# Attention with pooled keys and a mixture of adapters: the tail's last two chunks finished in halves, the last normalise in one piece

## The chip, the cores and the metric

The kernel runs on one core of a Trainium2 chip. The core has TensorE (PE) for matrix products, VectorE (DVE), ScalarE (ACT) and GpSimd (POOL) for elementwise work, and SyncE (SP), which issues most transfers; transfers run on 16 DMA engines. The metric is the device time of one execution in microseconds. The kernel before took 407.74 us, the median of four runs between 407.55 and 408.02.

## The reference

Two steps run one after the other. Keys and values are the same tensor: `kv` averaged over blocks of 4 x 4 positions and multiplied by `w_sr`. There are 4 batches of 12288 queries with 768 keys, all of width 128.

```
kv_pool = kv.reshape(B, H//4, 4, W//4, 4, C).mean(axis=(2, 4))
k = v = kv_pool.reshape(B, -1, C) @ w_sr
a = softmax(q @ k.T / sqrt(C));  x = (a @ v).reshape(B*S, C)

logits = x @ w_gate                         # 8 experts
topk, w = two largest logits, softmax over the two
out = x + sum over the two: w * ((x @ A[e]) @ B[e])     # rank 16
```

The output is 49152 x 128 in float32, 25 MB.

## The kernel before, in words

The queries are cut into 96 chunks of 512 rows, numbered 0 to 95; in the tail K stands for 95. A chunk has S = 4 slices of 128 rows, one row per partition. Chunks pass through these steps, each a function of the program:

- `scores`: TensorE multiplies the keys with 512 queries, ACT takes the exponential into `em` (L246).
- `attend`: for each slice, TensorE sums six products of `em` with `vx`, which holds 128 value columns, 8 columns of values already multiplied by `w_gate`, and a column of ones. The result in PSUM therefore holds the unscaled output, the unscaled logits and the row sum, 137 columns a slice.
- `normalize`: DVE takes the reciprocal of the row sums (L258) and multiplies the 4 x 136 other columns with it (L263). The result `xn` holds x and the logits.
- `top` and `route`/`gates`: DVE finds the largest logits (MAX8, L281), POOL and ACT form the gate weights `gw`; the softmax over two is written with a tanh (L312).
- `transposes`/`turn_x`: TensorE transposes x, a copy brings it out of PSUM.
- `down`, `gate`, `up`: the product with all eight A matrices side by side (128 columns), the multiplication by `gw` into `hg` on DVE, a transpose of `hg`, and the product with all B matrices.
- `finish`: DVE adds x (L360), SP issues the store of 256 KB.

The main loop works on several chunks at once, so that TensorE always has another chunk's product to do. The order is written out by hand: `keep` holds each instruction in program order on its engine, and a scheduler adds only the waits. Each engine works through its own list in order, so an instruction that waits holds up everything behind it on that engine. Pools of buffers recycle: an instruction that writes into a recycled buffer waits until the last reader of its former content is done. The pool of output buffers `osb` has 6 buffers, that of `tt1` 3, the PSUM pool `ps_m` 2 banks.

After the loop stands the tail, straight code for what is left of chunks K-4 to K. It spreads the work over the engines with its own helpers. `turn_x` and `turn_h` transpose into a PSUM bank, `fetch` copies the bank with ACT (L514), `down_into` and `up_into` multiply into a given bank. An output is finished in one of two ways: `carry` copies the bank to SBUF with ACT (L552) and `add_there` adds x on POOL and stores through SP (L556, L557), which is used for K-4 and K-3; `add_here` adds on DVE and stores through the queue it is given (L547, L548), which is used for K-2, K-1 and K.

Around the change, chunk K is treated apart. Its attention sum lies in the PSUM tile `o95`. The reciprocal is at L587; ACT scales two of its slices (L590), DVE scales the 8 logits of all slices into a tile of their own, `lg` (L593), and then the other two slices (L595). Its routing runs on DVE (L600 to L607, L620) with a tanh on ACT (L617). `gate_part` forms `hg` for a part of a chunk (L562): K-1 whole, ahead of K, and K in two halves of two slices. K-1's `hg` is turned and fetched whole; K's is turned in two halves, of which ACT copies one (L635) and DVE the other (L637). K-1 is then added and stored whole, and K in two halves, the first through ACT's queue and the second through SP's.

Of the kernel before, what the change touches and what calls it, by code (L numbers as in the profile page):

```python
# [10 lines left out]
FP32 = mybir.dt.float32  # L11
BF16 = mybir.dt.bfloat16
U16 = mybir.dt.uint16
FP16 = mybir.dt.float16
AF = mybir.ActivationFunctionType
ALU = mybir.AluOpType
# [4 lines left out]
def kernel(  # L21
# [10 lines left out]
    nc = tc.nc  # L32
    P = 128
    B, N, C = q.tensor.shape
    E, RK = 8, 16
# [3 lines left out]
    T = 512  # L39
    S = T // P  # L40
    GC = 4
    GT = GC * T
    VC = C + E
# [3 lines left out]
    scale = 1.0 / float(np.sqrt(C))  # L47
# [7 lines left out]
    xpool = ctx.enter_context(tc.tile_pool(name="xpool", bufs=5))  # L55
    rpool = ctx.enter_context(tc.tile_pool(name="rpool", bufs=4))
    gpool = ctx.enter_context(tc.tile_pool(name="gpool", bufs=6))
    run = ctx.enter_context(tc.tile_pool(name="run", bufs=3))
# [3 lines left out]
    ps_a = ctx.enter_context(tc.tile_pool(name="ps_a", bufs=1, space=bass.MemoryType.PSUM))  # L62
    ps_m = ctx.enter_context(tc.tile_pool(name="ps_m", bufs=2, space=bass.MemoryType.PSUM))

    keep = tc.keep_in_program_order

    def mm(*a, **k):
        return keep(nc.tensor.matmul(*a, **k))  # L68

    def mtile(shape, dtype=FP32, name="mb"):  # L70
        return ps_m.tile(shape, dtype, tag="mb", name=name)
# [71 lines left out]
    id_bf = const.tile([P, P], BF16)  # L143
# [90 lines left out]
    em, acc, xn, xg, srt, gw = {}, {}, {}, {}, {}, {}  # L234
    tts, xT, hgT, hp, hg, dp = {}, {}, {}, {}, {}, {}
# [20 lines left out]
    def normalize(k):  # L256
        ri = rpool.tile([P, S], FP32, tag="rinv", name="rinv")
        keep(nc.vector.reciprocal(ri, acc[k][:, :, VC]))  # L258
        k0, m = first[k], k - first[k]
        if m == 0:  # L260
            xg[k0] = xpool.tile([P, GC, S, VC], FP32, tag="xn", name="xn")
        x = xg[k0][:, m]
        keep(nc.vector.tensor_tensor(x, acc[k][:, :, 0:VC],  # L263
                                     ri.unsqueeze(2).broadcast_to([P, S, VC]), op=ALU.mult))
        xn[k] = x
# [129 lines left out]
    b_bf = const.tile([P, C], BF16)  # L395
# [21 lines left out]
    for k in range(LA, NCHUNK):  # L417
        b, i = divmod(k, NB)
# [70 lines left out]
    K = NCHUNK - 1  # L489
    assert kh == [K - 3] and ku == [K - 4], (kh, ku)  # L490

    def bank(pool):
        if pool is ps_m:
            return mtile([P, S, P], name="tail_ps")
        if pool is ps_a:
            return ps_a.tile([P, S, 256], FP32, tag="acc", name="acc")
        return ps_s.tile([P, 2, T], FP32, tag="sg", name="sg")
# [8 lines left out]
    def turn_h(k, pool):  # L506
        ps = bank(pool).bitcast(BF16).rearrange("p a b -> p (a b)")[:, 0:T].rearrange("p (s c) -> p s c", s=S)
        for s in range(S):
            mm(ps[:, s], hg[k][:, s], id_bf, is_transpose=True, start=(s == 0), stop=(s == S - 1))
        hgT[k] = ps  # L510

    def fetch(which, k):
        sb = run.tile([P, S, P], BF16, tag="tt1", name="tt1")
        keep(nc.scalar.copy(sb, which[k]))  # L514
        which[k] = sb

    def tanhs():
        for rest_ in later:
            rest_()
        later.clear()  # L520
# [7 lines left out]
    def wide(o):  # L528
        return o.rearrange("p a b -> p (a b)")[:, 0:T].rearrange("p (s c) -> p s c", s=S)
# [6 lines left out]
    def up_into(k, o):  # L536
        dp[k] = o
        for s in range(S):
            mm(o[:, s], hgT[k][:, s], b_bf, start=(s == 0), stop=(s == S - 1))

    def dest(k):
        return out[k // GC * GT:(k // GC + 1) * GT].rearrange("(p j) c -> p j c", p=P)[
            :, k % GC * S:(k % GC + 1) * S]

    def add_here(k, lo, hi, queue):
        osb = opool.tile([P, S, C], FP32, tag="osb", name="osb")[:, 0:hi - lo]
        keep(nc.vector.tensor_tensor(osb, dp[k][:, lo:hi], xn[k][:, lo:hi, 0:C], op=ALU.add))  # L547
        keep(queue.dma_start(dest(k)[:, lo:hi], osb))  # L548
# [6 lines left out]
    def add_there(k):  # L555
        keep(nc.gpsimd.tensor_tensor(dp[k], dp[k], xn[k][:, :, 0:C], op=ALU.add))  # L556
        keep(nc.sync.dma_start(dest(k), dp[k]))  # L557

    def gate_part(k, lo, hi):
        if lo == 0:  # L560
            hg[k] = run.tile([P, S, P], BF16, tag="hg", name="hg")
        keep(nc.vector.tensor_tensor(  # L562
            hg[k][:, lo:hi].rearrange("p s (e r) -> p (s e) r", e=E),
            hp[k][:, lo:hi].rearrange("p s (e r) -> p (s e) r", e=E),
            gw[k][:, lo:hi].rearrange("p s e -> p (s e)")
            .unsqueeze(2).broadcast_to([P, (hi - lo) * E, RK]), op=ALU.mult))
# [3 lines left out]
    o95 = bank(ps_s).rearrange("p a (b c) -> p (a b) c", c=256)  # L570
# [12 lines left out]
    gate_part(K - 2, 0, S)  # L583
    add_there(K - 4)

    ri = rpool.tile([P, S], FP32, tag="rinv", name="rinv")
    keep(nc.vector.reciprocal(ri, o95[:, :, VC]))  # L587
    xn[K] = xpool.tile([P, GC, S, VC], FP32, tag="xn", name="xn")[:, 0]
    for s in range(2):
        keep(nc.scalar.activation(xn[K][:, s, 0:C], o95[:, s, 0:C], AF.Copy, bias=0.0,  # L590
                                  scale=ri[:, s:s + 1]))
    lg = rpool.tile([P, S, E], FP32, tag="lg", name="lg")
    keep(nc.vector.tensor_tensor(lg, o95[:, :, C:VC], ri.unsqueeze(2).broadcast_to([P, S, E]),  # L593
                                 op=ALU.mult))
    keep(nc.vector.tensor_tensor(xn[K][:, 2:S, 0:C], o95[:, 2:S, 0:C],  # L595
                                 ri[:, 2:S].unsqueeze(2).broadcast_to([P, 2, C]), op=ALU.mult))
    tanhs()
    so = rpool.tile([P, S, 8], FP32, tag="so", name="so")
    for s in range(S):
# [8 lines left out]
                                 op=ALU.is_ge))  # L608
# [6 lines left out]
    fetch(xT, K)  # L615
    th = rpool.tile([P, S, E], FP32, tag="th1", name="th1")
    keep(nc.scalar.activation(th, arg, AF.Tanh, bias=0.0, scale=0.5))  # L617
    gate_part(K - 1, 0, S)
    gw[K] = gpool.tile([P, S, E], FP32, tag="gw1", name="gw1")
    keep(nc.vector.scalar_tensor_tensor(gw[K], th, 1.0, mask, op0=ALU.add, op1=ALU.mult))  # L620
    down_into(K, ps_s)
    fetch(hgT, K - 2)
    carry(K - 3)
    add_there(K - 3)
    gate_part(K, 0, 2)
    gate_part(K, 2, S)
    up_into(K - 2, wide(bank(ps_s)))
    turn_h(K - 1, ps_m)
    fetch(hgT, K - 1)
    ps = bank(ps_m).bitcast(BF16).rearrange("p a b -> p (a b)")[:, 0:T].rearrange("p (s c) -> p s c", s=S)  # L630
    hgT[K] = run.tile([P, S, P], BF16, tag="tt1", name="tt1")
    for lo in (0, 2):
        for s in range(lo, lo + 2):
            mm(ps[:, s], hg[K][:, s], id_bf, is_transpose=True, start=(s == lo), stop=(s == lo + 1))
    keep(nc.scalar.copy(hgT[K][:, 0:2], ps[:, 0:2]))  # L635
    add_here(K - 2, 0, S, nc.sync)
    keep(nc.vector.tensor_copy(hgT[K][:, 2:S], ps[:, 2:S]))  # L637
    up_into(K - 1, bank(ps_m))
    dp[K] = wide(bank(ps_a))
    for lo in (0, 2):  # L640
        for s in range(lo, lo + 2):
            mm(dp[K][:, s], hgT[K][:, s], b_bf, start=(s == lo), stop=(s == lo + 1))
    add_here(K - 1, 0, S, nc.sync)
    add_here(K, 0, 2, nc.scalar)
    add_here(K, 2, S, nc.sync)


# [28 lines left out]
```

The softmax here doesn't subtract the row's maximum and nothing guards it: scores larger than these inputs give would overflow.

## Time and profile before

| What | Value |
|---|---|
| median of four runs | 407.74 us (407.55 to 408.02) |
| the profiled execution: time | 407.72 us |
| the profiled execution: span, first to last instruction | 405.7 us |
| TensorE busy | 379.3 us, 94% of the span |
| DVE, ACT, POOL busy | 325.0, 292.2, 170.4 us |
| granted TensorE clock, mean | 0.995 |
| DMA, mean over the span | 188 GB/s |
| last arithmetic instruction | starts at 400.52, 0.41 us long |

The span counts from the first to the last instruction; some 2 us of the device time lie around it. A row of the timeline gives the start in us from the span's start, the length, the engine, the line, the operation, output and inputs with their shapes, and the idle time of the engine before it with the instruction that ended it. Rows of the same kind that follow each other are merged (x2): the length then covers them all. "SPq" is the issue of a transfer, not the transfer; a transfer's landing is the time from the issue to the last of its completion signals.

### The profile page before, as it was taken

What the parts mean: (1) busy time and instruction counts of PE and PEld (TensorE: products, weight loads), DVE (VectorE), ACT (ScalarE), POOL (GpSimd) and SP (SyncE); (2) the same over time, 40 slices, a digit from 0 to 9 for tenths busy, and PEclk for the clock granted to TensorE, in tenths of its full rate; (3) what the DMA queues carried; (4) which work ended last, traced back from release to release, by engine and by line L of the source; (5) the groups of instructions that cost most, each with busy time, mean ns of one, the idle gap of its engine ahead of it and who ended that gap; (6) DMA issues with size and microseconds to landing.
All of it is one profiled execution on the core that took longest, in us unless ns stands there. A gap on an engine that the chain in (4) does not pass through costs nothing.

```text
span 405.7 us, 11373 instructions
## 1 busy us (share of the span) xinstructions
PE 379.3 (94%) x4514; PEld 307.0 (76%) x4589; DVE 325.0 (80%) x950; ACT 292.2 (72%) x343; POOL 170.4 (42%) x289
## 2 busy tenths in 40 slices
PE   3898899999999999999999999999999999989893
PEld 2656778788887888788888888888888788777781
DVE  2553778888888888889888888889888888888874
ACT  2389468767687778767678778867678777666683
POOL 0010128788502318878412319779411313114242
PEclk9999999999999999999999999999999999999997
DMA  8997667994855999994844999994855645452213
GB/s 301 379 266 221 150 160 212 296 201 123 184 123 112 269 207 321 283 253 128 183 131 110 308 177 343 288 225 119 180 132 124 164 131 96 139 131 105 80 53 133
DMA packets 71319, 76.45 MB, mean 188 GB/s; under 512 B 49921, under 2 KB 50433, under 8 KB 70785
## 3 DMA queue, kind: packets, MB, share of 16 engines
q1 hardware_dynamic: 70128, 63.98, 54.1%
q0 software_dynamic: 704, 11.54, 16.4%
q8 instruction: 36, 0.59, 0.6%
q10 hardware_dynamic: 432, 0.20, 0.2%
q14 instruction: 19, 0.15, 0.1%
HBM read 50.53 MB, written 36.70 MB: 215 GB/s over the span
## 4 chain that ended last, share of the span: by engine, by line
PE 82%; DVE 7%; ACT 3%; DMA 3%; issue 2%; SPq 1%; POOL 1%; DVEq 0%; ACTq 0%; POOLq 0%
PE acc L68 34%; PE sg L68 23%; PE tt_ps L68 10%; PE h_ps L68 6%; PE d_ps L68 5%; ACT em L246 2%; DVE rinv L258 1%; DVE xn L263 1%; DMA w_sr_sb<-in_w_sr_dram 1%; SPq L98 1%; PE kpT_ps L68 1%; DMA kvr<-in_kv_dram 1%; DVE tts L333 1%; PE v_ps L68 1%; DVE hg L347 1%
## 5 line engine op out<-in xcount | busy, mean ns | idle before, releaser
L246 ACT ACTIVATE em<-sg 128x1024 f16<-128x1024 f32 x288 | 278.9, 1023 | 91.7 <-PE sg L68 59.9
L68 PE MATMUL acc<-vx,em 128*128 128x137 f16 x2280 | 171.6, 224 | 1.7 <-DVE xn L263 1.6
L68 PE MATMUL sg<-qT,kfT 128*128 128x512 bf16 x501 | 154.7, 378 | 2.7 <-ACT em L246 2.2
L68 PEld LDWEIGHTS <-em 128*128 128x128 f16 x2304 | 149.6, 98 | 4.0 <-DVE xn L263 2.2
L68 PEld LDWEIGHTS <-tts 128*128 128x128 bf16 x740 | 56.4, 98 | 45.8 <-DVE tts L333 2.1
L293 POOL TENSOR_TENSOR over<-xn,srt 128x128 f32<-128x128 f32 (+2 forms) x62 | 21.4, 363 | 157.1 <-DVE srt L281 157.1
L347 DVE TENSOR_TENSOR hg<-h_ps,gw 128x512 bf16<-128x512 f32 x93 | 64.2, 690 | 13.2 <-POOL gw L315 7.5
L263 DVE TENSOR_TENSOR xn<-acc,rinv 128x544 f32<-128x544 f32 x95 | 68.8, 724 | 3.3
L333 DVE COPY tts<-tt_ps 128x1024 bf16<-128x1024 bf16 (+1 forms) x96 | 64.4, 671 | 3.6 <-PE tt_ps L68 3.6
L171 POOL TENSOR_TENSOR kvr<-kvr 128x512 f32<-128x512 f32 x54 | 66.7, 1273 | 0.0
L360 DVE TENSOR_TENSOR osb<-d_ps,xn 128x512 f32<-128x512 f32 x91 | 62.5, 690 | 0.5 <-PE d_ps L68 0.5
L68 PEld LDWEIGHTS <-kfT 128*128 128x128 bf16 x576 | 45.8, 97 | 6.0 <-issue 3.7
L68 PEld LDWEIGHTS <-xn 128*128 128x128 bf16 x384 | 29.3, 98 | 21.9 <-DVE xn L595 0.5
L258 DVE RECIPROCAL rinv<-acc 128x4 f32<-128x4 f32 x95 | 17.2, 182 | 32.7 <-PE acc L68 31.5
L68 PE MATMUL h_ps<-a_bf,tts 128*128 128x128 bf16 x372 | 36.0, 219 | 2.8 <-DVE tts L333 1.6
L68 PE MATMUL tt_ps<-id_bf,xn 128*128 128x128 bf16 x372 | 35.9, 219 | 1.5
L68 PE MATMUL d_ps<-b_bf,tts 128*128 128x128 bf16 x364 | 35.2, 219 | 2.3 <-DVE tts L333 1.3
L68 PE MATMUL tt_ps<-id_bf,hg 128*128 128x128 bf16 x368 | 35.6, 219 | 0.3 <-DVE hg L347 0.3
L281 DVE MAX8 srt<-xn 128x8 f32<-128x8 f32 x380 | 34.2, 153 | 0.2
L314 POOL TENSOR_TENSOR gw<-th,over 128x128 f32<-128x128 f32 (+2 forms) x31 | 12.0, 387 | 37.1 <-ACT th L312 37.1
L68 PEld LDWEIGHTS <-hg 128*128 128x128 bf16 x384 | 25.4, 98 | 0.7 <-DVE hg L347 0.4
L169 POOL TENSOR_TENSOR kvr<-kvr 128x512 f32<-128x512 f32 (+1 forms) x18 | 18.1, 1004 | 0.9
(83 smaller groups left out, 174.5 us busy)
## 6 DMA issues: line engine op xcount, KB each, us to landing
out_dram<-osb SPq DMA_DIRECT2D x95, 256.0 KB, 3.4
kvr<-in_kv_dram SPq DMA_DIRECT2D x36, 512.0 KB, 6.5
qbf<-in_q_dram POOLq DMA_DIRECT2D x22, 512.0 KB, 5.9
kvr<-in_kv_dram SPq DMA_DIRECT2D x24, 256.0 KB, 5.1
qf<-in_q_dram SPq DMA_DIRECT2D x1, 1024.0 KB, 5.2
qf<-in_q_dram SPq DMA_DIRECT2D x4, 256.0 KB, 5.2
qT<-qbf SPq DMA_TRANSPOSE x22, 6.2
out_dram<-osb ACTq DMA_DIRECT2D x1, 128.0 KB, 3.4
```

What stands on the lines that cost most here:

```text
L68: return keep(nc.tensor.matmul(*a, **k))
L169: keep(adder.tensor_tensor(u, u, v, op=ALU.add))
L171: keep(adder.tensor_tensor(u[:, lo:hi], u[:, lo:hi], v[:, lo:hi], op=ALU.add))
L246: keep(nc.scalar.activation(em[k][:, 2 * r:2 * r + 2], ps, AF.Exp, bias=0.0, scale=scale))
L258: keep(nc.vector.reciprocal(ri, acc[k][:, :, VC]))
L263: keep(nc.vector.tensor_tensor(x, acc[k][:, :, 0:VC], ri.unsqueeze(2).broadcast_to([P, S, VC]), op=ALU.mult))
L281: keep(nc.vector.max(srt[k0][:, m, s], xn[k][:, s, C:VC]))
L293: keep(eng.tensor_tensor(d, lg, so[:, :, i].unsqueeze(2).broadcast_to([P, n, 8]), op=ALU.subtract))
L314: keep(eng.tensor_tensor(w[:, 0:n], th, mask, op=ALU.mult))
L333: keep(nc.vector.tensor_copy(sb[:, lo:hi], ps[:, lo:hi]))
L347: keep(nc.vector.tensor_tensor(hg[k].rearrange("p s (e r) -> p (s e) r", e=E), hp[k].rearrange("p s (e r) -> p (s e) r", e=E), gw[k0][:, m ...
L360: keep(nc.vector.tensor_tensor(osb, dp[k], xn[k][:, :, 0:C], op=ALU.add))
```

## The change

The change touches the tail alone. Chunk K is normalised by the `normalize` of all other chunks, over all four slices and the logits at once, and its routing reads the logits from there. The gates are formed in four halves, K's first. A loop then takes the four halves in the order K, K, K-1, K-1: each is transposed on TensorE and copied by ACT, and the up products, the additions and the stores are placed between them. K-2 is still added whole. K is added and stored in two halves on SP's queue, then K-1 in two halves, the first on ACT's queue and the second on SP's. K-1's output bank is taken after its halves have been turned, and its second up product comes in the program after the addition of its first half. There are seven tiles from the pool of output buffers in the tail where there were six.

```diff
-    ri = rpool.tile([P, S], FP32, tag="rinv", name="rinv")
-    keep(nc.vector.reciprocal(ri, o95[:, :, VC]))
-    xn[K] = xpool.tile([P, GC, S, VC], FP32, tag="xn", name="xn")[:, 0]
-    for s in range(2):
-        keep(nc.scalar.activation(xn[K][:, s, 0:C], o95[:, s, 0:C], AF.Copy, bias=0.0,
-                                  scale=ri[:, s:s + 1]))
-    lg = rpool.tile([P, S, E], FP32, tag="lg", name="lg")
-    keep(nc.vector.tensor_tensor(lg, o95[:, :, C:VC], ri.unsqueeze(2).broadcast_to([P, S, E]),
-                                 op=ALU.mult))
-    keep(nc.vector.tensor_tensor(xn[K][:, 2:S, 0:C], o95[:, 2:S, 0:C],
-                                 ri[:, 2:S].unsqueeze(2).broadcast_to([P, 2, C]), op=ALU.mult))
+    acc[K] = o95
+    normalize(K)
+    lg = xn[K][:, :, C:VC]
...
-    gate_part(K - 1, 0, S)
...
-    gate_part(K, 0, 2)
-    gate_part(K, 2, S)
+    halves = [(K, 0), (K, 2), (K - 1, 0), (K - 1, 2)]
+    for k, lo in halves:
+        gate_part(k, lo, lo + 2)
     up_into(K - 2, wide(bank(ps_s)))
-    turn_h(K - 1, ps_m)
-    fetch(hgT, K - 1)
-    ps = bank(ps_m).bitcast(BF16).rearrange("p a b -> p (a b)")[:, 0:T].rearrange("p (s c) -> p s c", s=S)
-    hgT[K] = run.tile([P, S, P], BF16, tag="tt1", name="tt1")
-    for lo in (0, 2):
+    dp[K] = wide(bank(ps_a))
+    turned = {k: bank(ps_m).bitcast(BF16).rearrange("p a b -> p (a b)")[:, 0:T]
+              .rearrange("p (s c) -> p s c", s=S) for k in (K - 1, K)}
+    for k in turned:
+        hgT[k] = run.tile([P, S, P], BF16, tag="tt1", name="tt1")
+
+    def half(ks, lo, lhs, rhs, transpose):
         for s in range(lo, lo + 2):
-            mm(ps[:, s], hg[K][:, s], id_bf, is_transpose=True, start=(s == lo), stop=(s == lo + 1))
-    keep(nc.scalar.copy(hgT[K][:, 0:2], ps[:, 0:2]))
-    add_here(K - 2, 0, S, nc.sync)
-    keep(nc.vector.tensor_copy(hgT[K][:, 2:S], ps[:, 2:S]))
-    up_into(K - 1, bank(ps_m))
-    dp[K] = wide(bank(ps_a))
-    for lo in (0, 2):
-        for s in range(lo, lo + 2):
-            mm(dp[K][:, s], hgT[K][:, s], b_bf, start=(s == lo), stop=(s == lo + 1))
-    add_here(K - 1, 0, S, nc.sync)
-    add_here(K, 0, 2, nc.scalar)
-    add_here(K, 2, S, nc.sync)
+            kw = dict(is_transpose=True) if transpose else {}
+            mm(ks[:, s], lhs[:, s], rhs, start=(s == lo), stop=(s == lo + 1), **kw)
+
+    for k, lo in halves:
+        half(turned[k], lo, hg[k], id_bf, True)
+        keep(nc.scalar.copy(hgT[k][:, lo:lo + 2], turned[k][:, lo:lo + 2]))
+        if (k, lo) == (K, 2):
+            half(dp[K], 0, hgT[K], b_bf, False)
+            add_here(K - 2, 0, S, nc.sync)
+        elif k < K:
+            if lo == 0:
+                half(dp[K], 2, hgT[K], b_bf, False)
+                add_here(K, 0, 2, nc.sync)
+                add_here(K, 2, S, nc.sync)
+    dp[K - 1] = bank(ps_m)
+    half(dp[K - 1], 0, hgT[K - 1], b_bf, False)
+    add_here(K - 1, 0, 2, nc.scalar)
+    half(dp[K - 1], 2, hgT[K - 1], b_bf, False)
+    add_here(K - 1, 2, S, nc.sync)
```

## The prediction, made before the result was known

> **What bounds the kernel now.** I read the page's engine table first, then the chain that ended last, then the tail as a timeline, then stretches of half a microsecond behind it, because the two programs' instruction lists are the same on every engine up to the reciprocal of chunk K = 95 at 394.65 us. TensorE carries the whole span, but nothing before 394.65 is touched, so the other 97% of the 405.7 us span is a constant here.
>
> ```profile
> span 405.7 us, 11373 instructions
> PE 379.3 (94%) x4514; PEld 307.0 (76%) x4589; DVE 325.0 (80%) x950; ACT 292.2 (72%) x343; POOL 170.4 (42%) x289
> PE 82%; DVE 7%; ACT 3%; DMA 3%; issue 2%; SPq 1%; POOL 1%; DVEq 0%; ACTq 0%; POOLq 0%
> ```
>
> The tail, row by row (start, length, engine, line): where chunk K is normalised in three pieces on two engines, where its routing starts, and where the last outputs are added and issued.
>
> ```profile
> 394.65 0.18 DVE L587 RECIPROCAL rinv<-sg 128x4 f32<-128x4 f32 x1
> 394.87 0.62 ACT L590 ACTIVATE xn<-sg,rinv 128x128 f32<-128x128 f32 x2
> 395.52 0.19 DVE L593 TENSOR_TENSOR lg<-sg,rinv 128x32 f32<-128x32 f32 x1 [0.69 <-ACT xn L590]
> 395.63 0.41 DVE L595 TENSOR_TENSOR xn<-sg,rinv 128x256 f32<-128x256 f32 x1
> 396.10 0.29 PE L68 MATMUL tail_ps<-id_bf,xn 128*128 128x128 bf16 x2 [0.33 <-DVE xn L595]
> 396.48 0.59 ACT L514 COPY tt<-tail_ps 128x512 bf16<-128x512 bf16 x1 [0.40 <-PE tail_ps L68]
> 396.90 0.69 DVE L562 TENSOR_TENSOR hg<-tail_ps,gw 128x512 bf16<-128x512 f32 x1
> 397.79 0.76 DVE L562 TENSOR_TENSOR hg<-sg,gw 128x256 bf16<-128x256 f32 x2
> 398.23 1.27 POOL L556 TENSOR_TENSOR osb<-osb,xn 128x512 f32<-128x512 f32 x1 [1.37 <-ACT osb L552]
> 399.53 0.33 SPq L557 DMA_DIRECT2D out_dram<-osb  x1
> 400.19 0.74 DVE L547 TENSOR_TENSOR osb<-acc,xn 128x256 f32<-128x256 f32 x2
> 400.43 1.01 SPq L548 DMA_DIRECT2D out_dram<-osb  x1
> ```
>
> The last arithmetic ends at 400.93, yet the span runs to 405.7. Stretches of that rest (window, length, the engines' busy time, clock, DMA share, GB/s):
>
> ```profile
> 400.00:400.50 0.50, 0.02 (x1) 0.00 (x0) 0.50 (x2) 0.00 (x0) 0.00 (x0) 1.00 0.23 90
> 400.50:401.00 0.50, 0.00 (x0) 0.00 (x0) 0.43 (x2) 0.00 (x0) 0.00 (x0) 1.00 1.06 393
> 402.50:403.00 0.50, 0.00 (x0) 0.00 (x0) 0.00 (x0) 0.00 (x0) 0.00 (x0) 0.50 1.01 363
> 403.00:403.50 0.50, 0.00 (x0) 0.00 (x0) 0.00 (x0) 0.00 (x0) 0.00 (x0) 0.50 0.14 47
> DMA to landing us min/median/max: 2.9/2.9/2.9
> ```
>
> What to see: from 400.4 to 403.0 all sixteen DMA engines are full at 363 to 416 GB/s, with the outputs of chunks K-3 to K, 4 x 256 KB. That is 1.05 MB in 2.7 us, so the last four stores form one saturated stream that begins 0.83 us after K-3's issue at 399.53. After 403.0 a trickle of 25 to 47 GB/s goes on to about 404.1: one engine that carried an 8 KB instruction fetch (issued at 400.52, 0.75 us long, in the packets) finishes its share a microsecond after the rest. The landing line is the last store's: issued 401.53, landed about 404.5. From there to the end of the span are 1.2 us of closing waits and barriers. So the end is set by the start of the stream and its bytes, and by the last issue only where that comes late.
>
> **The change, part by part.** The profiled execution took 407.72 us (span 405.7 and 2.0 around it), 0.02 under the median of 407.74, so one sum serves both.
>
> *Whole normalise.* Two ACT pieces (0.62), the logits piece (0.19) and the half normalise (0.41) go; one DVE pass over 128x544 comes, 0.72 us by the same form at 392.49. It starts 0.22 after the reciprocal, as there: 394.87 to 395.60, against 396.04 for the last piece before. TensorE turns all four slices from 395.66 (hand-off 0.06, as 396.04 to 396.10) at 0.056 each; the last starts at 395.83 instead of 396.17: 0.34 earlier. Before, two slices were already turned at 395.29 and 395.54; losing that lead costs 0.10 of the 0.44 gained. ACT loses 0.62 of work, so the tanh of K-1 (395.38) starts near 394.65, but POOL is inside its 1.27 us add from 395.01 and forms the gates at 396.23 to 396.86 as before: no gain there. The rest moves with the 0.34: ACT's copy of xT 396.48 to 396.14, K's tanh 396.96 to 396.62 (its argument, three small DVE rows behind the four MAX8 at 395.63, is done by 396.43), the copy for K-2 397.09 to 396.75, the carry of K-3 397.56 to 397.22, POOL's add 398.23 to 397.89, and K-3's issue on SP 399.53 to 399.19. POOL is free for it at 396.86.
>
> *Gates in halves, K first.* K-1's 0.69 us gate no longer stands on DVE ahead of K's: K's first half starts with TensorE's down product, 397.22 instead of 397.79. Four halves at 0.33 apart (0.76 for two ending 0.41 after the second start) run to 398.64. DVE's add for K-2 follows at 398.56, 0.10 later than before; its issue waits behind K-3's anyway (399.61 against 399.95).
>
> *The ping-pong.* Each half is turned on TensorE (two matmuls, 0.29), copied on ACT (0.37, row at 398.98), and only then is the next half turned into the same bank: the new program has a wait for ACT's copy in front of the second half of both chunks. Hand-offs are 0.31 from the last matmul's start to ACT and 0.06 back. K: turned 397.70, copied 398.08 to 398.45, turned 398.51, copied 398.89 to 399.26, up product 399.32 to 399.60. DVE adds K's halves at 399.64 and 399.97. K-1: turned 398.76, copied 399.16 to 399.53, turned 399.59, copied 399.96 to 400.33. Its first add goes at 400.30 (DVE free) to 400.71; the second up product now waits for that add, because it writes the bank being read: 400.77 to 401.05; last add 401.09 to 401.51. So the last arithmetic ends 0.58 later than the 400.93 of before. The new wait inside one bank has no row in this trace; its bounds are zero (if only disjoint halves were guarded) and the two copies it exposes, 2 x (0.37 + 0.06) = 0.86. I take the chain above, since the waits stand in the built program.
>
> *Seven output buffers in a pool of six.* The last add also waits for K-4's store, issued 396.30 and landed 3.4 later, 399.7: covered by 1.4 us. That cover is gone only if the store lands after 401.1.
>
> *Stores.* SP issues K-3, K-2, K's two halves, K-1's second half, with ACT issuing K-1's first at about 400.74. Bytes are the same; SP has one issue more. Rows for an issue go from 0.33 to 1.01 (the one at 400.43). With 0.4 each, K's halves go at 400.09 and 400.6 and K-1's last at 401.55, as soon as it is added. With 1.01 for both, it goes at 402.2.
>
> *Where it ends.* The stream starts 0.34 earlier and holds the same bytes and, I assume, the same instruction fetch on DVE's count of instructions (one fewer in all, so it stays in the tail): the last landing moves from 404.5 to 404.14. The last issue alone gives 401.55 plus a landing: 2.0 us for an undisturbed 256 KB store at 390.84, 2.9 for the last half of before: 403.55 to 404.45. The later of both is 404.14 to 404.45; I take 404.2, nearer to the stream, since a half store that meets a draining stream queues less than the 2.9 row did. Then one closing wait fewer follows it (0.06). Sum: -0.3 - 0.06, about -0.35: 407.4 us. The bounds: -0.9 if the fetch hold is gone and the last issue lands in 2.0; +0.7 with both slow issues and 2.9.
>
> The Trainium skill (DMA: Bandwidth & Descriptors, section "Anatomy of one DMA — SWDGE (gpsimd) path") speaks against halves: about 2.0 us fixed for each DMA plus bytes over 436 GB/s, fitted on the GpSimd path. By it, as an estimate, a 128 KB half takes 2.3 us, the last would land at 403.85 and the sum would be 407.0; two halves would cost a second fixed part, but beside the first. The four last landings of this trace, 2.9 to 3.8 us, show queueing on top of any fixed part, and the sum above goes by them.
>
> **The rivals.** *A: the later arithmetic decides (slower).* Mechanism: SP's third and fourth output issues are held for 1.01 us each like the one at 400.43, so K-1's last half is issued at 402.2. For it: that row, and the issues of 0.60 in a row while the first loads saturate the queues. Against it: the issue right after the long one took 0.41. With a landing of 2.9 it ends at 405.1, +0.6: 408.3. With the 3.4 of ACT's half it gives 405.6, +1.1: 408.8. It decides from an issue later than about 401.6 and passes 0.2% from 402.4 with 2.9.
>
> *B: the stream drains early (faster).* If the fetch falls before the stream, or the earlier K halves fill it better, the slow engine ends with the others (403.1 before, 402.8 now), the last half lands at 403.5 to 403.7: -0.8 to -1.0, 406.7 to 406.9. For it: the 1 us of trickle is one fetch's work. Against it: DVE's instruction count puts the fetch near its last adds, which come later now.
>
> *C: the split is hidden on both sides.* 0.34 won and 0.58 lost meet at the DMA: a landing of 2.9 after 401.55 gives 404.45, no change: 407.7.
>
> **How the numbers follow.** What this measurement can tell from no change is 0.2%, 0.82 us. The forecast (407.1 to 407.6) gets 0.47, C 0.23, A 0.17 (somewhat over half of it past 408.56), B 0.13. Faster by over 0.2% (under 406.92): 0.13 of B and a little of the forecast's edge, 0.15. Slower: 0.10. Within: 0.75. The range 406.8 to 408.3 leaves out the far part of A and half of B.
>
> **What would show it.** In the new profile: one 0.72 us normalise of K ending near 395.6 with no ACT row beside it; K-3's issue near 399.2; DVE's last four adds of 0.41, the last two apart by about 0.8 with TensorE between them, the last ending near 401.5; the full DMA stretch starting near 400.0 instead of 400.4, and the trickle ending near 403.8. I am wrong if K-3's issue does not move (the normalise was not what held it), if an SP issue of about a microsecond stands ahead of the last one, or if the trickle is missing.

## The result and the profile after

The changed kernel took 407.22 us (median of 41 runs, 406.68 to 407.83) against 407.72 us (61 runs). The ratio is 0.9987 with a 95% interval of 0.9983 to 0.9991: 0.5 us faster, 0.3 to 0.7. That is within the 0.2% that the forecast counted as no change, and clear of zero. Its profiled execution has a span of 405.4 us against 405.7.

The timeline of the changed kernel's tail, for the rows that answer to those of before (start, length, engine, line, operation, idle time before it):

```profile
394.71 0.18 DVE L258 RECIPROCAL rinv<-sg 128x4 f32<-128x4 f32 x1
394.92 0.72 DVE L263 TENSOR_TENSOR xn<-sg,rinv 128x544 f32<-128x544 f32 x1
395.70 0.40 PE L68 MATMUL tail_ps<-id_bf,xn 128*128 128x128 bf16 x4 [0.23 <-DVE xn L263]
397.27 0.75 DVE L562 TENSOR_TENSOR hg<-sg,gw 128x256 bf16<-128x256 f32 x2
397.95 1.27 POOL L556 TENSOR_TENSOR osb<-osb,xn 128x512 f32<-128x512 f32 x1 [1.07 <-ACT osb L552]
398.55 0.27 PE L68 MATMUL tail_ps<-id_bf,hg 128*128 128x128 bf16 x2 [0.52 <-ACT tt L633]
399.24 0.33 SPq L557 DMA_DIRECT2D out_dram<-osb  x1
399.67 2.25 SPq L548 DMA_DIRECT2D out_dram<-osb  x4
400.75 0.35 PE L68 MATMUL tail_ps<-b_bf,tt 128*128 128x128 bf16 x2 [0.81 <-DVE osb L547]
401.13 0.42 DVE L547 TENSOR_TENSOR osb<-tail_ps,xn 128x256 f32<-128x256 f32 x1 [0.44 <-PE tail_ps L68]
```

The whole tail stands 0.06 us later in this execution (the reciprocal at 394.71, not 394.65), so from here on times are counted from that reciprocal's start, R, as the trace gives them. One pass normalises chunk K with no ACT row beside it. K-3's store is issued at R+4.54 instead of R+4.88. The two new waits are there, 0.52 us for ACT's copy and 0.81 us for DVE's add, and the last add ends at R+6.85 instead of R+6.28.

Half-microsecond stretches of the changed kernel, two around its last adds and three at the end (window, length, busy time of PE, PEld, DVE, ACT and POOL, clock, DMA share, GB/s):

```profile
400.00:400.50 0.50, 0.00 (x0) 0.10 (x1) 0.50 (x3) 0.24 (x1) 0.00 (x0) 1.00 0.86 336
400.50:401.00 0.50, 0.25 (x2) 0.10 (x1) 0.20 (x1) 0.00 (x0) 0.00 (x0) 0.81 1.03 393
402.50:403.00 0.50, 0.00 (x0) 0.00 (x0) 0.00 (x0) 0.00 (x0) 0.00 (x0) 0.50 0.72 246
403.00:403.50 0.50, 0.00 (x0) 0.00 (x0) 0.00 (x0) 0.00 (x0) 0.00 (x0) 0.50 0.06 23
403.50:404.00 0.50, 0.00 (x0) 0.00 (x0) 0.00 (x0) 0.00 (x0) 0.00 (x0) 0.50 0.06 18
```

The stretch from 400.0 carries 336 GB/s, where before it carried 90: the stream of the last stores begins earlier, fills the same 2.7 us, and the trickle on one engine is still behind it. An instruction fetch is still in it too: in the window R+5.3 to R+9.6 the DMA queues of this kernel have

```profile
q14 instruction: 1, 0.01, 0.6%
```

From R to the span's end the old kernel takes 11.00 us and the new one 10.71.

### The profile page after: what moved, and what is told of

Its sections match the earlier page's. It is cut to its first block, busy times and chain, and to the rows that moved or that the text cites. A ratio compares the mean times of both kernels' runs of the same rounds, so it can differ in the third digit from the quotient of the medians.

```text
span 405.4 us, 11373 instructions
## 1 busy us (share of the span) xinstructions
PE 378.9 (93%) x4514; PEld 306.9 (76%) x4589; DVE 325.3 (80%) x950; ACT 292.2 (72%) x343; POOL 170.4 (42%) x289
## 4 chain that ended last, share of the span: by engine, by line
PE 82%; DVE 7%; ACT 3%; DMA 3%; issue 2%; SPq 1%; POOL 1%; DVEq 0%; ACTq 0%; POOLq 0%
PE acc L68 34%; PE sg L68 23%; PE tt_ps L68 10%; PE h_ps L68 6%; PE d_ps L68 5%; ACT em L246 2%; DVE xn L263 2%; DVE rinv L258 1%; SPq L98 1%; DMA kvr<-in_kv_dram 1%; DMA w_sr_sb<-in_w_sr_dram 1%; PE kpT_ps L68 1%; DVE tts L333 1%; PE v_ps L68 1%; DVE hg L347 1%
```

## The experiments

All times are medians beside runs of the kernel before on the same chip (407.68, 407.73 and 407.87 us in the three jobs). Every run also has a profile, and the tail in it, from R to the span's end, tells more than the medians: it leaves out the 394 us that no experiment touches, in which R itself fell anywhere from 393.9 to 395.0. Each kernel has one profile; two pairs of kernels that end in the same way have tails 0.01 and 0.02 us apart (10.09 and 10.10, 10.37 and 10.39).

**Each part alone.** `norm_only` is the kernel before with the whole normalise:

```diff
-    (the three pieces of the normalise, with lg)
+    acc[K] = o95
+    normalize(K)
+    lg = xn[K][:, :, C:VC]
```

> Only the whole normalise of chunk K; everything else as before. Theory S (the end is set by the store stream, which begins with the issue of K-3's store, by its bytes and by the instruction fetch on one DMA engine): the issue of K-3 moves from 399.53 to about 399.2 and the end with it, -0.3 us against before, so about 407.4, or 0.2 us above the full change. Rival H (the halves carry the gain): within 0.1 us of before, 407.7.

Measured: 407.31 us, ratio 0.9991 (0.9982 to 1.0); the tail 10.63 against 11.00. The issue of K-3 stands at R+4.54:

```profile
393.94 0.18 DVE L258 RECIPROCAL rinv<-sg 128x4 f32<-128x4 f32 x1
398.47 0.33 SPq L557 DMA_DIRECT2D out_dram<-osb  x1
```

That is what theory S expected of the kernel before. Against the full change it expected 0.2 us more; the median is 0.09 above and the tail 0.08 below it.

`halves_only` is the changed kernel with the three pieces put back:

```diff
-    acc[K] = o95
-    normalize(K)
-    lg = xn[K][:, :, C:VC]
+    (the three pieces of the normalise, with lg)
```

> The halves and their stores as in the change, but chunk K normalised in three pieces as before. Theory S: the issue of K-3 stays near 399.53, the last add ends later than in the change (near 401.8), and the time is that of before within 0.15 us, 407.6 to 407.85. Rival L (the end is the issue of the last half store plus about 2.7 us): the last issue near 401.85 is 0.3 later than both kernels had, so 408.0. Rival H: most of the 0.5 us gain is here, 407.2.

Measured: 407.11 us, ratio 0.9985 (0.9976 to 0.9993), the tail 10.26. K-3's issue (R+4.88) and the late last issue (R+7.25) are as S and L said, yet it is the fastest tail of the four so far. S and L both failed here, and H alone had the number. The trace had the reason: the trickle is gone. The DMA queues in the window R+5.3 to R+9.6 (queue, kind, packets, MB, share of 16 engines), first of the kernel before, then of `halves_only`:

```profile
q1 hardware_dynamic: 576, 0.92, 56.6%
q10 hardware_dynamic: 144, 0.13, 8.8%
q14 instruction: 1, 0.01, 1.1%
```

```profile
q1 hardware_dynamic: 723, 0.92, 58.1%
q10 hardware_dynamic: 144, 0.13, 8.8%
```

The stores move the same bytes, but no instruction fetch falls among them. The last 8 KB fetch before the end starts at R+5.87 before, at R+6.52 in the changed kernel, and at R+4.68 here, ahead of the stream. The three kernels differ by an instruction or two on DVE (1094, 1093 and 1095 in their traces). So this comparison mixed the halves with the place of a fetch.

**The fetch by itself.** Fourteen one-column memsets on DVE, in a stretch at the start where it waits 5 us for the first transfer, move everything that DVE fetches 14 instructions forward in its list and cost no time of their own (a kernel that has them is called padded from here on):

```diff
     nc.vector.memset(warm, 0.0)
+    pad = const.tile([P, 1], FP32)
+    for _ in range(14):
+        keep(nc.vector.memset(pad, 0.0))
```

> The full change, with 14 one-column memsets on DVE behind the first one, where DVE waits 5 us for the first transfer. They move DVE's instruction fetches 14 instructions earlier in its list, so the one at 401.23 falls near 397, ahead of the store stream. Theory S with the fetch as the cause of the trickle: the last landing moves from 404.3 to about 403.5, the time from 407.2 to about 406.4. Theory S without it (the slow engine is slow by itself), or rival L: 407.2 within 0.15.

Measured: 406.75 us, ratio 0.998 (0.9971 to 0.9989); tail 10.10 against 10.71. The fetch moved to R+0.72 and the last landing from R+9.60 to R+8.99. The direction is that of theory S with the fetch as the cause, called theory F from here on; the size is 0.6 us, not 0.8.

> The kernel before, with the 14 memsets. The instruction fetch leaves the store stream. Theory F (the trickle behind the stream is that fetch on one engine): the last landing moves from 404.5 to about 403.7, 0.8 us, so 406.9. Rival (the memsets help the changed kernel alone, or the gain of the padded change was chance): 407.7 within 0.2. Under F the padded change is then only 0.1 to 0.2 us faster than this kernel, against 0.5 without the memsets.

Measured: 407.0 us, ratio 0.9983 (0.9973 to 0.9992); tail 10.39 against 11.00, again 0.61. The padded change is 0.29 us shorter in the tail than this kernel, a little more than the 0.1 to 0.2 expected. In the window R+5.3 to R+9.6 the same bytes are stored as in the kernel before, without an instruction fetch:

```profile
q1 hardware_dynamic: 576, 0.92, 57.0%
q10 hardware_dynamic: 144, 0.13, 8.7%
```

Half-microsecond stretches of this kernel, where the trickle was:

```profile
402.74:403.24 0.50, 0.00 (x0) 0.00 (x0) 0.00 (x0) 0.00 (x0) 0.00 (x0) 0.50 0.96 338
403.24:403.74 0.50, 0.00 (x0) 0.00 (x0) 0.00 (x0) 0.00 (x0) 0.00 (x0) 0.50 0.18 57
403.74:404.24 0.50, 0.00 (x0) 0.00 (x0) 0.00 (x0) 0.00 (x0) 0.00 (x0) 0.50 0.00 0
```

The stream runs full to 403.2 and stops. That the trickle is one engine is in the completion signals: a store has sixteen, and the last store of the kernel before had fifteen of them by R+9.04 and the sixteenth at R+9.83; here they are in by R+9.20 and R+9.21.

`before_pad3` has `range(3)` in place of `range(14)`:

> The kernel before with 3 memsets instead of 14. Theory F: DVE's fetch moves three instructions, from 5.87 after the reciprocal to between 4.3 and 5, ahead of the stream's first bytes at 5.71, and almost all of the 0.6 to 0.7 us that 14 memsets gave is there: 407.0 to 407.1, the span from the reciprocal to the end 10.4. Rival (the shift has to be large, or the memsets act otherwise): 407.5 to 407.7, 11.0.

Measured: 407.18 us, ratio 0.9989 (0.998 to 0.9997); the fetch at R+4.34, the tail 10.37. Three instructions do what fourteen did. In all thirteen traces one 8 KB fetch begins when DVE has begun 1080 to 1090 of its instructions.

The other way round, `halves_late` moves three small DVE instructions of the start to POOL, so that the fetch comes later in the list:

```diff
-    nc.vector.memset(warm, 0.0)
+    nc.gpsimd.memset(warm, 0.0)
-    nc.vector.tensor_copy(id_bf, id_f)
+    nc.gpsimd.tensor_copy(id_bf, id_f)
-    nc.vector.tensor_copy(wext[:, 0:C], w_sr_sb)
+    nc.gpsimd.tensor_copy(wext[:, 0:C], w_sr_sb)
```

> The halves alone with the old normalise, but three small DVE instructions of the start (the first memset and two copies) moved to POOL, where it idles. That puts DVE's fetch three instructions later in its list, back among the last adds, 6 us or more behind the reciprocal. Theory F (the halves alone were 0.6 us faster only because two more DVE instructions had pushed the fetch ahead of the stream): the trickle returns and the time rises by 0.5 to 0.8, to 407.6 to 407.9. Rival H (the halves themselves gain): stays at 407.1.

Measured: 407.41 us, ratio 0.9991 (0.9982 to 1.0); tail 10.86 against 10.26 for the same halves without the move. Its queues in the window R+5.3 to R+9.6, and two stretches behind the stream:

```profile
q14 instruction: 1, 0.01, 0.4%
```

```profile
403.38:403.88 0.50, 0.00 (x0) 0.00 (x0) 0.00 (x0) 0.00 (x0) 0.00 (x0) 0.50 0.10 33
403.88:404.38 0.50, 0.00 (x0) 0.00 (x0) 0.00 (x0) 0.00 (x0) 0.00 (x0) 0.50 0.05 16
```

The fetch is back at R+7.33, the trickle is back, and 0.60 us of tail with it; the median, up by 0.30, stays under the 407.6 to 407.9 expected. Rival H, that most of the gain comes from the halves, falls: with a fetch in the stream they leave the tail 0.14 us shorter than the kernel before.

**The whole normalise without the fetch.** `norm_pad14` is `norm_only` with the 14 memsets.

> Whole normalise alone, with the 14 memsets. Theory F and S together (no fetch in the stream, the stream begins 0.34 earlier, the last store is issued 6.3 us after the reciprocal and no longer sets the end): 0.3 us under the padded kernel before and 0.2 under the padded change, 406.55. Rival L (without the fetch the end is the last issue plus 1.9 us): 0.6 under the padded kernel before, 406.3. Rival H (the halves are needed): no better than the padded kernel before, 406.9.

Measured: 406.79 us, ratio 0.9975 (0.9964 to 0.9986); tail 10.05, 0.34 under the padded kernel before as expected, but only 0.05 under the padded change where 0.2 was expected. This is the shortest tail of the kernels that compute everything. It closes a table of tails in us:

| | fetch in the stream | fetch ahead of it |
|---|---|---|
| kernel before | 11.00 | 10.39 |
| whole normalise alone | 10.63 | 10.05 |
| halves alone | 10.86 | 10.26 |
| both (the change) | 10.71 | 10.10 |

The fetch is worth 0.58 to 0.61 us in every row, whatever else is in the kernel. The other two do not add up. The whole normalise gains 0.37 and 0.34 us without the halves, but 0.15 and 0.16 with them; the halves gain 0.14 and 0.13 us on the old normalise and lose 0.08 and 0.05 on the new one. So in these tails the halves bring the change nothing; the medians, which lie the other way by 0.09 us without the memsets and 0.04 with them, cannot tell. Why the halves and the whole normalise interact was not tested.

**The last issue.** `own_bank` gives K-1's second up product another bank:

```diff
     add_here(K - 1, 0, 2, nc.scalar)
+    dp[K - 1] = wide(bank(ps_s))
     half(dp[K - 1], 2, hgT[K - 1], b_bf, False)
```

> The full change, but the second up product of K-1 goes to a bank of its own, so that it no longer waits 0.8 us for the addition of the first half. The last add ends near 401.05 instead of 401.55 and the last store is issued 0.45 earlier. Theory S: no more than 0.1 us, 407.1 to 407.2. Rival L: -0.45, 406.8.

Measured: 407.07 us, ratio 0.9986 (0.9977 to 0.9995); the last add ends at R+6.34 instead of R+6.85, the last store is issued at R+6.44 instead of R+6.88, and the tail is 10.77 against 10.71. Rows of the last two adds:

```profile
399.86 0.41 DVE L547 TENSOR_TENSOR osb<-tail_ps,xn 128x256 f32<-128x256 f32 x1
400.20 0.42 DVE L547 TENSOR_TENSOR osb<-sg,xn 128x256 f32<-128x256 f32 x1
```

They now follow each other with no wait, and nothing comes of it: the last landing is R+9.64, against R+9.60. Rival L falls where the fetch is in the stream. One row of this trace is unlike the others, the last issue:

```profile
400.72 0.74 SPq L548 DMA_DIRECT2D out_dram<-osb  x1
```

It began 0.02 us before the fetch (R+6.46), and the 1.01 us issue of the kernel before began 0.09 us before its fetch. But the issues that began 0.07 and 0.08 us before the fetch in `halves_late` and `norm_only` took 0.33 us, so a fetch alone does not make an issue long.

> The full change with a bank of its own for K-1's second up product, and the 14 memsets. Without the fetch the padded change ended 1.9 us after its last issue (7.09 after the reciprocal), so here that issue counts: 0.5 earlier, but then the stream sets the end near 8.6 to 8.7 after the reciprocal. Theory: 0.3 to 0.4 us under the padded change, 406.4. Rival (the last issue never counts, as in the run of its own bank without memsets, 0.1 us): 406.7.

Measured: 407.1 us, ratio 0.9984 (0.9976 to 0.9993); last issue R+6.44 against R+7.09, last landing R+8.98 against R+8.99, tail 10.09 against 10.10. The expectation was wrong: also without the fetch the last issue does not count. The medians of these two equal tails lie 0.35 us apart, which tells how far a median of 11 runs can be trusted here. The pair with and without the fetch, `own_bank` and this kernel, tells the same: its tails differ by 0.67 us (10.77 and 10.09), its medians by nothing (407.07 and 407.1).

**Bytes and start.** `no_store` is `norm_pad14` without the store of chunk K-3:

```diff
-        keep(nc.sync.dma_start(dest(k), dp[k]))
+        if k != K - 3:
+            keep(nc.sync.dma_start(dest(k), dp[k]))
```

> Whole normalise with the 14 memsets, but the store of chunk K-3 (256 KB) is left out, so that these rows of the output are not written; all arithmetic and the last issues stay. Theory S (the stream's start and bytes set the end): K-2's store opens the stream and 768 KB are left; the last landing moves from 8.88 after the reciprocal to about 8.2, where the last issue (6.27) plus 1.9 takes over; 0.6 to 0.7 us faster than with the store, about 406.1. Rival L (last issue plus a fixed 2.6): no change.

Measured: 406.11 us (5 runs), ratio 0.9965 (0.9952 to 0.9978); the tail 9.81 against 10.05 and the last landing R+8.57 against R+8.88, while the last issue stayed at R+6.26. K-2's store, now the first, is issued at R+4.47. Stretches of this kernel:

```profile
400.39:400.89 0.50, 0.00 (x0) 0.00 (x0) 0.50 (x3) 0.00 (x0) 0.00 (x0) 0.50 0.93 365
400.89:401.39 0.50, 0.00 (x0) 0.00 (x0) 0.23 (x1) 0.00 (x0) 0.00 (x0) 0.50 0.14 53
401.39:401.89 0.50, 0.00 (x0) 0.00 (x0) 0.00 (x0) 0.00 (x0) 0.00 (x0) 0.50 1.01 377
```

L (no change) falls again, but S was half off, although the median met its 406.1: the tail gave 0.25 us of the 0.6 to 0.7. The stream has a hole from 401.0 to 401.3 (R+6.1 to R+6.4). K-2's store drains before K-1's, issued at R+5.60, arrives. So not only the first store can set the end but any of them, with the bytes behind it. With 0.83 us from issue to first byte and 390 GB/s: K-3 gives 4.54 + 0.83 + 2.69 (1.05 MB) = 8.06 with the store, K-1 gives 5.60 + 0.83 + 1.34 (0.52 MB) = 7.77 without it. The difference of 0.29 is near the 0.31 measured. This rule was made after the run. In the eight traces without DVE's fetch in the stream the last landing (in `dve_add` that of fifteen engines) comes 0.73 to 0.92 us behind the largest such sum, so the rule is good to some 0.2 us. It fails by that much between `after_pad14` and `own_bank_pad14`: in the first the last half store has the largest sum, 7.09 + 0.83 + 0.34 = 8.26, in the second K-3's store, 8.06, and both landed at the same moment.

The last test of this group, `dve_add`, adds K-3's output on DVE instead of ACT's copy and POOL's add, in `norm_pad14`:

```diff
-    carry(K - 3)
-    add_there(K - 3)
     gate_part(K, 0, 2)
     gate_part(K, 2, S)
+    add_here(K - 3, 0, S, nc.sync)
```

> Whole normalise with the 14 memsets, and K-3's output added by DVE right behind K's gates instead of by ACT's copy and POOL's 1.27 us add. All bytes and the last issues stay; K-3's store is issued near 4.15 after the reciprocal instead of 4.54. Theory S: the stream begins 0.4 earlier and the last landing follows by 0.3 to 0.4, from 8.88 to about 8.55: 406.4. Rival L: no change, or later by up to 0.1 where DVE's extra 0.6 us delays the last add.

Measured: 407.16 us, ratio 0.9985 (0.9976 to 0.9994); tail 10.29, 0.24 longer. Both parts of the expectation missed. K-3 is issued at R+4.47, not R+4.15, because K's gates start only behind K-1's whole gate in this order (R+3.09, where the change has R+2.56). And K-1's store now leaves at R+5.86, so the rule above gives 5.86 + 0.83 + 1.34 = 8.03 against 8.06, nothing gained; on fifteen of the sixteen engines the last store indeed landed by R+8.86. The sixteenth landed at R+9.12: the fetch that stood at R+4.43 now stands at R+7.92, inside the stream. ACT has 451 instructions in this trace against 455, POOL 364 against 368. The counts point to ACT: in all thirteen traces an 8 KB fetch begins when ACT has begun 447 to 450 of its instructions, and here it comes to number 448 only at R+7.92. No run moved this fetch on purpose, so its owner is argued, not shown.

## Why the prediction was right

Its sum was -0.35 us, made of -0.3 at the landing and -0.06 for a closing wait. In the two profiles the last landing moved by 0.23 us (R+9.83 to R+9.60) and the rest behind it shrank by 0.06, so the tail shrank by 0.29 us; the medians moved by 0.50 (0.3 to 0.7). Step by step:

- **Whole normalise.** It forecast K-3's issue 0.34 us earlier; it is 0.34 earlier (R+4.88 to R+4.54). `norm_only` shows that this alone brings the gain: 0.37 us of tail.
- **The ping-pong.** It forecast the last add 0.58 later (0.57 measured) and the two waits, one of which the trace of before did not show. That the wait for DVE's add costs nothing at the end is shown by `own_bank`. No run took away the wait for ACT's copy.
- **Stores.** SP's issues took 0.33 to 0.41 us; the long issue of rival A did not come. The 1.01 us row of before came in the tail of none of the eleven experiments, and one of 0.74 us in `own_bank`; what makes them is open.
- **The end.** It put the last landing at 404.2, R+9.55; measured R+9.60. Its sum left the last half store 2.65 us from issue to landing; measured 2.72. The 2.3 us that it named beside the sum came in neither case: 2.72 with the fetch in the stream, 1.90 without (`after_pad14`). It said that the stream and not the last issue sets the end, which `own_bank` and `own_bank_pad14` show, and `no_store` with the correction that a later store can take the first one's place. The 0.06 for a closing wait came as forecast: from the last landing to the span's end it is 1.17 to 1.18 us in the kernels without halves that write every output and 1.11 to 1.12 in those with them.
- **The fetch.** It assumed that the fetch stays among the stores because DVE's list changes by one instruction. It did, at R+6.52, and DVE's list is indeed what places it. But the margin was small: two DVE instructions more put it ahead of the stream in `halves_only`. Rival B, the stream without the fetch, was priced at 0.8 to 1.0 us; the runs show 0.6. That term was oversized because the trickle's whole length was counted, while the other fifteen engines land later when the sixteenth no longer waits: the last store's fifteenth signal came at R+9.04 with the fetch and at R+9.20 without it on the kernel before, at R+8.79 and R+8.97 on the changed one.
- **Size.** The forecast of 407.4 is a little short of the measured gain. The 0.2 us between the tail's 0.29 and the medians' 0.50 is not located. Over the ten experiments that write every output, the gain in the medians lies between 0.28 us below and 0.37 us above the gain in the tails.

## What to carry to other kernels

At the end of a kernel, look for the first moment at which the stores saturate the DMA engines: for each store add its issue, the time to its first byte and the bytes still to come, and work on the one with the largest sum, since a later last add may cost nothing. That rule was made from these traces and holds in them to some 0.2 us. Before a gain of half a microsecond is put down to an edit, look where the instruction fetches fall in both traces: a change of two instructions on one engine can move a fetch into or out of the last stores. Compare the stretch that was edited in the traces, because the rest of a 400 us run moves by more than such a gain.

## What the runs showed of the hardware that was not expected

An 8 KB instruction fetch (0.3 to 0.75 us long in the packets) that falls among the last stores held one of the sixteen DMA engines: the last store's sixteenth completion signal came 0.59 to 0.85 us behind the fifteenth in the five traces with DVE's fetch in the stream, and 0.01 to 0.03 us behind it in the seven without any. It lengthened the tail of the profiled execution by 0.58 to 0.67 us in five pairs of kernels. The medians of these pairs, each taken against the kernel before of its job, differ by 0.0 to 0.7 us the same way. Where it falls followed DVE's instruction count: three one-column memsets at the start, in idle time, moved it from R+5.87 to R+4.34 and shortened the tail of the kernel before by 0.63 us, more than the change under study did. A half store of 128 KB issued last, at the end of a full stream, landed in 1.9 us in the padded change and in 2.5 us when issued 0.65 us earlier: it arrived at the same moment.
